# Turning more attention output by DMA, in a kernel whose order a planner writes

## The chip, the cores and the metric

The kernel runs on one core of a Trainium2 chip. A core has TensorE (PE, with its weight loads shown as PEld), VectorE (DVE), ScalarE (ACT), GpSimd (POOL) and SyncE (SP); POOL, SP and ACT also issue DMAs, which 16 DMA engines carry out. The metric is the device time of one execution in microseconds (us), of which the median over runs is compared.

## The reference

Two stages, the second fed by the first. Sizes: 8 batches, 8 heads, 576 positions, head width 64; then 4608 tokens, width 512, 8 experts, inner width 1024.

```python
def phi(x):
    proj = np.einsum('bhsd,df->bhsf', x, w_phi)
    proj = proj - np.max(np.abs(proj), axis=-1, keepdims=True)
    return np.concatenate([np.exp(proj), np.exp(-proj)], axis=-1)
q_p, k_p = (phi(q), phi(k))
kv = np.einsum('bhsf,bhsd->bhfd', k_p, v)
z = np.sum(k_p, axis=2)
num = np.einsum('bhsf,bhfd->bhsd', q_p, kv)
den = np.einsum('bhsf,bhf->bhs', q_p, z)[..., None] + 1e-06
attn_out = num / den
x = attn_out.transpose(0, 2, 1, 3).reshape(B * S, H * D)

logits = x @ w_gate
P = np.exp(logits - logits.max())
for _ in range(8):
    P /= P.sum(1, keepdims=True) + 1e-09
    P /= P.sum(0, keepdims=True) + 1e-09
    P *= N / E
for e in range(E):
    h = np.maximum(x @ w1[e], 0.0)
    out += P[:, e:e + 1] * (h @ w2[e])
```

## The kernel before

Every operation is first recorded in a `Plan`, with its engine, a duration and what it reads and writes; `Plan.schedule` then plays the record through. At each step it starts, of all operations that are ready, the one that can start first, and among equals the one with the lowest number (`idx`, its place in the record plus `plan.prio`). The order that comes out is the order of instructions in each engine's queue. On the chip each queue runs strictly in that order, and semaphores hold an instruction until what it reads is there. The planner's durations therefore set the order but not the times.

**Attention.** The 8 heads of a batch make 4 pairs, so there are 32 pairs, numbered 4 x batch + pair. The string `order` lists the steps of the attention, one letter each, in the order in which they are recorded:

- `l`, `e`: load halves of a batch, and its last 64 positions. From batch 2 on q and k come through POOL's queue.
- `t`: turn a half's q and k with a DMA transpose on SP's queue (L567, 512 KB). `r` does it for the last 64 positions (L686).
- `a`, `q`, `p`: project and take exponentials on ACT (L618), with the maxima on DVE (L614).
- `b`, `n`, `m`: sums over keys, then the quotient, on PE (L622, L905) and DVE (L913, L918, L919). The result of a pair is the tile `xb`.
- `c` (`pair_c`): turn `xb` so that tokens lie along the free axis, into `xT`. For batches 3 to 6 this is a DMA transpose of 128 KB on SP's queue (L928). For the others PE turns four 128x128 blocks (L934) and DVE copies the result from PSUM (L937).
- `g`: turn the last 64 positions of all four pairs on PE (L944), copy them (L949), and compute the gate's logits of the group of 512 tokens.
- `w`: load expert 0's weights in eight parts through POOL's queue (L527, L531).
- `u`, `d`: the expert work that fills the attention's gaps: expert 0's up product of a group with its relu on ACT (L983, tile `hx`), and its down product with a copy into `acc`.

Some tiles lie inside larger ones, and the profile shows the larger name: `wx` stands for part of the buffers of `xb`, `k` and others, too.

**Routing.** The eight normalisations are a chain on DVE, with one small matmul each (L622 `ps<-cs,colw`), while PE goes on with expert 0.

**Experts 1 to 7.** The products use Strassen-like sums: DVE forms sums of weights and of tokens (L1240), PE multiplies (L1475, L1607, L1466), ACT and DVE empty the banks (L1527, L1530, L1535, L1676, L1860, L1872), POOL adds into `acc` (L1875). For experts from 2 on some products are split once more; `fine_up` forms the finer weight sums (`step`, 256 elements each), into space inside `xT`. Sums of tokens are written to DRAM in expert 1's turn (L1385, L1422, L1450) and read back later (L1397). The order of the small units of work inside a turn is written out in `UNITS`, one line for each kind of turn.

The planner prices a DMA by two numbers: how long its queue is held, and how long the transfer takes:

```python
o = plan.op(queue, 0.8 if queue == "POOL" else 0.6, 0.0, fn, r, w, (), nbytes / speed)
o.turn, o.unit = rate == 148, unit
```

Of the kernel before, what the change touches and what calls it, by code (L numbers as in the profile page):

```python
# [12 lines left out]
ALU = mybir.AluOpType  # L13
# [113 lines left out]
class Links:  # L127
# [13 lines left out]
    def step(self, t, work):  # L141
        on = [n for n in range(2) if self.line[n] and self.line[n][0][0] <= t + 1e-9]
        later = [x[0][0] for n, x in enumerate(self.line) if x and n not in on]
        if not on:
            return (min(later), None, None) if later else None
        share = [1.0, 1.0]
        if len(on) == 2:
            a, b = (x[0][2] for x in self.line)
            all_ = (0.61 if a.turn else 0.84) / (a.unit + b.unit)
            share = [all_ * a.unit, all_ * b.unit]  # L150
        dt, n = min((work[n] / share[n], n) for n in on)
        if later and later[0] - t < dt:
            dt, n = max(later[0] - t, 0.0), None
        for i in on:
            work[i] -= dt * share[i]
        return t + dt, n, work
# [193 lines left out]
def kernel(  # L350
# [18 lines left out]
    NP = H // 2  # L369
# [40 lines left out]
    plan = Plan()  # L410
# [17 lines left out]
    def dma(queue, nbytes, rate, fn, r=(), w=()):  # L428

        speed, unit = LINK.get(rate, (rate, 40))  # L430
        if nbytes == 2 << 20:
            speed, unit = 400, 150
        o = plan.op(queue, 0.8 if queue == "POOL" else 0.6, 0.0, fn, r, w, (), nbytes / speed)
        o.turn, o.unit = rate == 148, unit

    TI, GR, KM, QM, PM, NM, RM = 0, 0, 0, 0, 0, 0, 0
# [69 lines left out]
    def new(tag):  # L506
        return R[tag].new()
# [416 lines left out]
        return xb, outs  # L924

    def pair_c(b, pr, xb):
        if b in (3, 4, 5, 6,):
            dma("SP", 1 << 17, 148, lambda: nc.sync.dma_start_transpose(  # L928
                out=xT[:, pr, b * SM:(b + 1) * SM].rearrange("p (a c) -> p a c", c=128),
                in_=xb()[:, 0:NJ].rearrange("p a b -> p (a b)")), [(xb, 0), (xb, 1)], [("xT", b, pr)])  # L930
            return
        pxt = new("PP")
        for j in range(NJ):
            pe(128, lambda j=j: nc.tensor.transpose(  # L934
                bf(pxt)[:, j * 128:j * 128 + 128], xb()[:, j, :], ident),
                [(xb, 0), (xb, 1), "ident"], [pxt])
        dve(270, lambda: nc.vector.tensor_copy(  # L937
            out=xT[:, pr, b * SM:(b + 1) * SM], in_=bf(pxt)[:, 0:512]),
            [pxt], [("xT", b, pr)])
# [91 lines left out]
    for b in range(2):  # L1031
# [4 lines left out]
        w=["wphi_f0"])  # L1036
    dma("ACT", 1 << 15, 100, lambda: nc.scalar.dma_start(out=wphi_f[64:128, :], in_=w_phi),
        w=["wphi_f1"])
# [13 lines left out]
    for i in range(2):  # L1052
        dve(450, lambda i=i: nc.vector.memset(vrd[i], 0.0),
            w=[("vrd", i, h, *y) for h in range(2) for y in ((), (1,))])
# [35 lines left out]
    def stage_g(b):  # L1090
# [9 lines left out]
             "c": lambda j: pair_c(j // 4, j % 4, xbs[j]), "g": stage_g,  # L1100
             "u": lambda i: up0(i // 4, i % 4), "d": lambda i: down0(i // 4, i % 4)}
    order = (
        "lraeaepqbwlqaqawwabwmqlltnrbppnwqbppmrmanbqaqmwwacmpnpbccpwbtcnmqnaqbclupunm"
        "taumquglcapalbcpnqqdcenmucugbblnapmrcqdutabnqpmunpbambccddnqplanmqmducpblttb"
        "augnaqlnrbdcampcadmqeutunqcppmdcaqtdqabpbbmlrqtdnpmuaqualbnagnacctbmqulupran"
        "tdpmtdqcmdnpdabdancpcabbqmpumqbcdgnappqunburqcbugmmnqdcdanumupqbnucmcpnmbddp"
        "bqmpncncubncmmgccg"
    )
    for i, n in enumerate(order):
        at[0] = i  # L1110
# [23 lines left out]
    o = plan.op("X", 0.0, 0.0, swap, w=["late"])  # L1134
# [136 lines left out]
    def fine_up(A, n):  # L1271

        f, r = A[n]
        t, key, first = FINE_W[n]

        def a(q, k):
            return lambda: f()[:, k, :].rearrange("p (f q c) -> p q f c", f=2, q=2)[:, q]

        def s(n):
            return lambda: t()[:, n]  # L1280

        def step(n, x, y, op, r, w):
            sub(dve, 256, s(n), x, y, op, r, [(key, n), *w])

        step(0, a(1, 0), a(1, 1), ALU.add, r, first)
        step(2, a(0, 0), a(1, 0), ALU.subtract, r, [])
        step(1, s(0), a(0, 0), ALU.subtract, [*r, (key, 0)], [])
        step(3, a(0, 1), s(1), ALU.subtract, [*r, (key, 1)], [])
        A[n + "*"] = t, [(key, i) for i in range(4)]
# [500 lines left out]

    def down7(e, g, H, B7):

# [131 lines left out]

    END = "X1 p2 Y1 X2 Z1 p3 X3 Z2 X4 p0 p1".split()
    UNITS = [o.split() for o in (
# [27 lines left out]
    turns = [int(i) for i in (  # L1954
        "0 1 2 3 4 5 6 7 8 9 10 11 12 13 14 15 16 17 9 10 11 12 13 14 15 16 17 9 10 11 12 "
        "13 14 15 16 17 9 10 11 12 13 14 15 16 17 9 10 11 12 13 14 15 16 17 18 9 10 11 12 "
# [22 lines left out]
    for e in range(1, E):  # L1979
        w1, w2 = load_w(e, ["late", ("acc", 4, 0, 0)] if e > 1 else ["late"])  # L1980
        if e == 1:
            nextX = sums_x(pairs[0])
        A7 = sums_up(e, w1)
        B7 = sums_down(e, w2) if e > 1 else None
        turn = [*pairs, (8,)] if e < E - 1 else [(8,), *pairs]
        if e == 2:
            o = plan.op("X", 0.0, 0.0, lambda: None, w=["K"])
            for d in plan.ops[:-1]:
                if any(b.ring is R["X"] for b in d.bufs):
                    d.users.append(o)  # L1990
                    o.deps.append(d)
                    o.left += 1
        for n, gs in enumerate(turn):
            if (e, n) == (1, 4):
                plan.inorder = 1
            X = nextX if e == 1 else load_fine(gs)
            H = {g: [] for g in gs}
            for fp in range(len(gs)):
                hs = take()
                for i, z in enumerate(hs):  # L2000
                    H[gs[min(i, len(gs) - 1)]].append(z)
                fine = e > 1 and len(gs) == 2
                if fine:
                    un = up49(A7, fp, X, H, gs, ["up0", "K"])
                else:
                    un = up7(A7, gs, fp, X, H, ["up0"])
                for o in UNITS[turns.pop(0)]:
                    if o in un:
                        un[o]()
                    elif len(o) == 3:  # L2010
                        un[o[:2], int(o[2])]()
                    elif dn is not None:
                        dn[o]()
                if dn is not None:
                    dn["out"]()
                    slots.extend(dn["slots"])
                if e == 1 and fp == 0 and n + 1 < len(turn):
                    nextX = sums_x(turn[n + 1], [(H[gs[0]][0], 0, 1, 1)])
                if B7 is None and fp:
                    B7 = sums_down(e, w2)  # L2020
                if fp == len(gs) - 1:
                    wait += [(e, g, H[g], B7, w2, [z.ring.number for z in H[g]]) for g in gs]
                dn = next_down()
# [35 lines left out]
```

## Time and profile before

| | |
|---|---|
| median of 3 runs | 1010.16 us (1009.79 to 1010.67) |
| profiled execution | span 1008.8 us from the first to the last instruction; its time outside the span is not listed, the median is 1.4 us above it |
| PE, PEld busy | 994.0 us (99%), 727.7 us (72%) |
| DVE, ACT, POOL busy | 898.6 us (89%), 812.8 us (81%), 447.6 us (44%) |
| granted TensorE clock | 1.000 |
| DMA | 128.86 MB, mean 128 GB/s |

Busy time of PE is the union of its matmuls, whose ends are modelled and overlap, so the time from one start to the next tells its pace better than the length of one. `SPq` is SP's queue: the time that an issuing instruction held it, waits included. A row of the windows table gives the length of a stretch, and for each engine the busy time in it and the number of instructions, then the granted clock, the DMA share (which counts overlapping queues, so it can exceed 1) and GB/s.

### The profile page before, as it was taken

The page shows a single profiled execution, that of the slowest core. Times are in us where ns is not written, and L with a number is a line of the kernel's source. Part 1 is how long each engine was busy: PE and PEld are TensorE (multiplying, and loading weights), DVE is VectorE, ACT ScalarE, POOL GpSimd, SP SyncE. Part 2 cuts the span into 40 slices and gives each one's busy share as a digit, 9 for nine tenths or more (in the row PEclk, how much of TensorE's full clock was granted, in tenths as well). Part 3 has the DMA queues.
Part 4 walks back from the last instruction along what each step waited for, and adds up shares of the span by engine and source line. Part 5 has one row for each costly group of instructions (what it writes and reads, how often), then busy time and mean ns, then how long its engine had stood idle before and what let it go on. Part 6 is the DMA issues. An engine that isn't in the chain of part 4 may idle for free.

```text
span 1008.8 us, 23309 instructions
## 1 busy us (share of the span) xinstructions
PE 994.0 (99%) x8376; PEld 727.7 (72%) x8376; DVE 898.6 (89%) x1999; ACT 812.8 (81%) x1930; POOL 447.6 (44%) x514
## 2 busy tenths in 40 slices
PE   7899999999999999999999999999999999999998
PEld 5666666644566877777777877787778777787775
DVE  7999998987888998899989898989889988989886
ACT  7999999845979788878878788777887888778874
POOL 5778674400133344434444444444443444344443
PEclk9999999999999999999999999999999999999999
DMA  9999999181136423282327133632246222724653
GB/s 249 183 202 183 157 153 144 38 170 56 53 121 143 147 97 98 84 184 96 109 98 170 44 100 131 130 127 98 97 117 177 97 98 84 147 79 142 208 174 126
DMA packets 129748, 128.86 MB, mean 128 GB/s; under 512 B 55776, under 2 KB 98272, under 8 KB 129632
## 3 DMA queue, kind: packets, MB, share of 16 engines
q1 hardware_dynamic: 97680, 103.33, 36.3%
q0 software_dynamic: 31648, 23.86, 16.9%
q8 instruction: 65, 1.06, 0.5%
q14 instruction: 51, 0.42, 0.2%
q10 hardware_dynamic: 304, 0.20, 0.1%
HBM read 122.50 MB, written 19.53 MB: 141 GB/s over the span
## 4 chain that ended last, share of the span: by engine, by line
PE 92%; DVE 3%; ACT 2%; DMA 2%; issue 1%; POOL 0%; DVEq 0%
PE ps L1466 41%; PE ps L1475 20%; PE ps L622 17%; PE ps L1607 11%; PE ps L905 2%; DMA xi6t<-X 1%; DMA xi<-X 1%; PE ps L752 1%; ACT q L618 0%; DVE m L614 0%; ACT k L618 0%; DVE wx L614 0%; DVE X L1240 0%; DMA acc<-in_k_dram 0%; DVE hs L1676 0%
## 5 line engine op out<-in xcount | busy, mean ns | idle before, releaser
L1875 POOL TENSOR_TENSOR acc<-acc,hx 128x512 f32<-128x512 f32 x186 | 236.1, 1276 | 404.7 <-ACT hx L1872 135.0
L1466 PEld LDWEIGHTS <-hs 128*128 128x128 bf16 x1984 | 194.1, 98 | 46.4 <-issue 0.2
L1872 ACT ACTIVATE hx<-ps,P 128x256 f32<-128x256 f32 x372 | 158.9, 483 | 53.4 <-PE ps L1466 52.0
L1860 DVE SCALAR_TENSOR_TENSOR acc<-ps,P,acc 128x256 f32<-128x256 f32 x372 | 162.2, 478 | 30.2 <-PE ps L1466 28.2
L1475 PE MATMUL ps<-xT,T 128*128 128x512 bf16 x608 | 171.0, 379 | 0.0
L1466 PEld LDWEIGHTS <-hx 128*128 128x128 bf16 x1488 | 145.6, 98 | 24.9
L1466 PE MATMUL ps<-hx,hs 128*128 128x256 bf16 x992 | 144.3, 273 | 0.0
L1676 DVE CUSTOM_DVE_ANT_0 hs<-ps,U 128x512 bf16<-128x512 f32 x192 | 124.7, 684 | 11.3 <-PE ps L1475 6.6
L1607 PE MATMUL ps<-xT 128*128 128x256 bf16 x576 | 125.4, 272 | 0.0
L1475 PEld LDWEIGHTS <-T 128*128 128x128 bf16 x672 | 65.8, 98 | 40.6
L1682 ACT ACTIVATE hs<-ps 128x512 bf16<-128x512 f32 x96 | 55.9, 598 | 41.7 <-PE ps L1475 40.2
L1466 PE MATMUL ps<-wx,hs 128*128 128x256 bf16 x560 | 78.4, 273 | 0.0
L622 PE MATMUL ps<-w,hx 128*128 128x512 bf16 x288 | 73.0, 379 | 0.0
L622 PE MATMUL ps<-xT,w 128*128 128x512 bf16 x288 | 72.9, 379 | 0.0
L1466 PE MATMUL ps<-wx,hx 128*128 128x256 bf16 x496 | 72.3, 273 | 0.0
L1676 DVE CUSTOM_DVE_ANT_0 hs<-ps,X 128x512 bf16<-128x512 f32 x96 | 65.1, 684 | 7.8 <-PE ps L1607 6.9
L1466 PE MATMUL ps<-hx 128*128 128x256 bf16 x496 | 71.2, 273 | 0.0
L1607 PEld LDWEIGHTS <-xT 128*128 128x128 bf16 x576 | 56.3, 98 | 17.5
L1466 PE MATMUL ps<-w,hx 128*128 128x256 bf16 x432 | 62.2, 273 | 0.0
L614 DVE TENSOR_REDUCE m<-ps 128x4 f32<-128x512 f32 x88 | 58.8, 680 | 3.7 <-PE ps L622 1.9
L1672 ACT COPY X<-ps 128x512 f32<-128x512 f32 x96 | 58.6, 610 | 2.5 <-DVE ps L1650 2.5
L1466 PE MATMUL ps<-w,hs 128*128 128x256 bf16 x432 | 60.2, 273 | 0.0
(174 smaller groups left out, 2256.0 us busy)
## 6 DMA issues: line engine op xcount, KB each, us to landing
xT<-xi SPq DMA_DIRECT2D x48, 448.0 KB, 4.6
xT<-xd SPq DMA_DIRECT2D x72, 256.0 KB, 4.0
wx<-in_moe_w_dram POOLq DMA_DIRECT2D x8, 1024.0 KB, 11.2
v_m<-in_v_dram SPq DMA_DIRECT2D x15, 512.0 KB, 5.2
out_dram<-acc SPq DMA_DIRECT2D x14, 512.0 KB, 3.0
w<-in_moe_w_dram POOLq DMA_DIRECT2D x6, 1024.0 KB, 11.0
xT<-xp SPq DMA_DIRECT2D x24, 256.0 KB, 2.8
qk<-in_k_dram POOLq DMA_DIRECT2D x12, 256.0 KB, 5.4
```

The costliest lines, as they stand in the source:

```text
L614: dve(el, lambda: nc.vector.tensor_reduce(out=dst(), in_=src(), axis=AX.X, op=ALU.max, apply_absolute_value=True), r, w)
L622: nc.tensor.matmul(out_, lhsT=lhsT, rhs=rhs, start=start, stop=stop)
L905: pe(65, lambda j=j: nc.tensor.matmul(pn()[:, j * D1:j * D1 + D1], lhsT=s["T"][x]()[:, j % 2, 2 * h + j // 2, :] if j < 4 else r["T"][x]() ...
L1466: pe(256, lambda i=i, k=k, z=z: nc.tensor.matmul(bank()[:, 256 * i:256 * i + 256], lhsT=lhs(k, i), rhs=rhs(k), start=first and z, stop=k = ...
L1475: pe(512, lambda k=k: nc.tensor.matmul(bank().rearrange("p (a b) -> p a b", a=2), lhsT=lhs(k), rhs=rhs(k), start=first and k == 0, stop=k ...
L1607: pe(256, lambda: nc.tensor.matmul(halves_of(bank[q], n)(), lhsT=lhs(), rhs=t()[:, rhs, :], start=start, stop=True, skip_group_check=True) ...
L1672: act(512, lambda: nc.scalar.copy(out=flat(to[q])(), in_=bank[q]()), [bank[q]], [(to[q], 0), (to[q], 1)])
L1676: dve(515, lambda: nc.vector._custom_dve(ADD_SAT, out=out_(q, i, j), in0=bank[q]().rearrange("p (a b) -> p a b", a=2), in1=to[q](), s0=3.0 ...
L1682: act(512, lambda: nc.scalar.activation(out=out_(q, i, j), in_=bank[q]().rearrange("p (a b) -> p a b", a=2), func=ACT.Relu, bias=0.0, scal ...
L1860: dve(320, lambda n=n, ts=ts: nc.vector.scalar_tensor_tensor(out=acc[g][:, ts, 256 * j:256 * j + 256], in0=bank()[:, 256 * n:256 * n + 256 ...
L1872: act(370, lambda n=n: nc.scalar.activation(out=u()[:, n, :], in_=bank()[:, 256 * n:256 * n + 256], func=ACT.Copy, bias=0.0, scale=P[:, 4 ...
L1875: pool(695, lambda: nc.gpsimd.tensor_tensor(out=acc[g][:, 2 * i:2 * i + 2, 256 * j:256 * j + 256], in0=acc[g][:, 2 * i:2 * i + 2, 256 * j: ...
```

## The change

Four edits.

1. The planner now holds SP's queue for 2.8 us for a turn of 512 KB and for 1.25 us for a smaller one, where it held 0.6 us.
2. `pair_c` turns all pairs by DMA but 0 to 3, 6 and 7: 26 of 32 where it was 16. Newly turned by DMA are pairs 4 and 5 (batch 1), 8 to 11 (batch 2) and 28 to 31 (batch 7).
3. The `order` string and all 19 lines of `UNITS` are other permutations of the same steps and units. The weight sums of expert 2 (`sums_up`, `fine_up`) get numbers lower by 300, so that they win ties against the rest.
4. In `fine_up` the third sum also waits for the space in `xT` to be free.

```diff
-        o = plan.op(queue, 0.8 if queue == "POOL" else 0.6, 0.0, fn, r, w, (), nbytes / speed)
+        issue = 0.8 if queue == "POOL" else 0.6
+        if rate == 148:
+            issue = 2.8 if nbytes == 1 << 19 else 1.25
+        o = plan.op(queue, issue, 0.0, fn, r, w, (), nbytes / speed)
         o.turn, o.unit = rate == 148, unit
...
     def pair_c(b, pr, xb):
-        if b in (3, 4, 5, 6,):
+        if NP * b + pr not in (0, 1, 2, 3, 6, 7):
             dma("SP", 1 << 17, 148, lambda: nc.sync.dma_start_transpose(
...
     order = (
-        "lraeaepqbwlqaqawwabwmqlltnrbppnwqbppmrmanbqaqmwwacmpnpbccpwbtcnmqnaqbclupunm"
+        "laapqewrqlaqewabwablbqwpnlmqbpcmrntmpraqbnwnaqppanmcpcbtwmcnbwpacqwqnlmuluua"
...
         step(0, a(1, 0), a(1, 1), ALU.add, r, first)
-        step(2, a(0, 0), a(1, 0), ALU.subtract, r, [])
+        step(2, a(0, 0), a(1, 0), ALU.subtract, r, first)
...
     UNITS = [o.split() for o in (
-        "x10 X1 x11 Y1 w10 Z1 Z2 X2 x21 x20 X3 w11 x30 x40 X4 y11 x31 w20 x41 y10 w21",
+        "x10 w10 y10 x11 X1 x21 X2 Z1 x20 w11 X3 Z2 w21 Y1 x31 w20 y11 x30 X4 x40 x41",
...
+        plan.prio = -300 if e == 2 else 0
         A7 = sums_up(e, w1)
+        plan.prio = 0
```

More of the change, by code (lines that the diff above doesn't have):

```diff
@@ L1102 @@
     order = (
-        "lraeaepqbwlqaqawwabwmqlltnrbppnwqbppmrmanbqaqmwwacmpnpbccpwbtcnmqnaqbclupunm"
[L1104 to L1107, printed above, removed]
+        "laapqewrqlaqewabwablbqwpnlmqbpcmrntmpraqbnwnaqppanmcpcbtwmcnbwpacqwqnlmuluua"
+        "mqbpmltuabgadalpbeccncmnucmupqqnptubgbaqrdnaqpquamtmpblnddccqapblpanmbtmddqn"
+        "pmdacbmrnuuatpgeqbubncnnmlctqpcbdlmudacclrnadpmqtbgutqlbndcpamatqucbanuqqapm"
+        "mcbubarundpqdmbpnqqdtpddanpmamqubgapqqurbncuanpbcdncmcmubadpmccbcqbungpqucmn"
+        "pdncbmdpnmncmucgcg"
     )
```

52 rows, old and new, of the table UNITS are left out of this document.

## The prediction

> **What bounds the kernel.** I read the page first: span, busy times, slices, and the summary of the chain that ended last.
>
> ```profile
> span 1008.8 us, 23309 instructions
> PE 994.0 (99%) x8376; PEld 727.7 (72%) x8376; DVE 898.6 (89%) x1999; ACT 812.8 (81%) x1930; POOL 447.6 (44%) x514
> PEclk9999999999999999999999999999999999999999
> DMA  9999999181136423282327133632246222724653
> PE 92%; DVE 3%; ACT 2%; DMA 2%; issue 1%; POOL 0%; DVEq 0%
> ```
>
> PE is busy in 994.0 of 1008.8 us at full clock, and 92% of the last chain is PE. Whether PE is truly full I take from the pace of matmuls in the chain (start, length, count):
>
> ```profile
> 81.53 1.73 PE ps L622 x8
> 331.61 17.47 PE ps L1466 x160
> 1001.93 3.06 PE ps L622 x22
> ```
>
> Eight matmuls of 512 columns take 1.73 us, 0.216 each; 160 of 256 columns take 17.47, 0.109 each: the same time per column early and late, with nothing between them. So PE is the bound, and only two things can move the end: PE work, and the time in which PE stands still. The windows table (length; PE, PEld, DVE, ACT, POOL busy with counts; clock, DMA share, GB/s) shows where it stands still:
>
> ```profile
> 0.00:64.00 64.00, 54.27 (x594) 37.77 (x595) 57.88 (x127) 58.31 (x145) 45.28 (x80) 1.00 1.17 216
> 64.00:196.00 132.00, 132.00 (x1524) 86.24 (x1523) 121.11 (x278) 127.38 (x312) 86.80 (x138) 1.00 0.98 145
> 196.00:245.00 49.00, 48.64 (x335) 24.09 (x334) 42.31 (x122) 20.45 (x39) 1.94 (x4) 1.00 0.44 94
> 245.00:350.00 105.00, 104.37 (x713) 69.60 (x712) 90.45 (x216) 89.87 (x179) 29.45 (x23) 1.00 0.43 122
> 350.00:1009.00 659.00, 654.70 (x5216) 509.99 (x5213) 586.81 (x1260) 516.83 (x1260) 284.15 (x271) 1.00 0.41 119
> 24.00:32.00 8.00, 6.99 (x81) 4.86 (x79) 7.88 (x19) 7.96 (x22) 5.50 (x10) 1.00 1.22 254
> 48.00:56.00 8.00, 7.63 (x101) 5.27 (x98) 7.96 (x21) 8.00 (x22) 7.81 (x12) 1.00 1.21 187
> ```
>
> PE idles 9.73 us in the first 64 us, 0.36 from 196 to 245, 0.63 from 245 to 350, and 4.30 after that, of which 4.0 follow the last matmul (1001.93 + 3.06 = 1004.99). Beyond the start there is one microsecond to win back. In the start ACT and DVE are full (7.96 and 7.88 of 8 us; 8.00 and 7.96), so PE waits for them. And from 64 to 196 us, the attention's main part, ACT is busy 127.38 of 132: PE and ACT are both nearly full there.
>
> **The change part by part.** The order listing of both programs shows what is issued: 40 transposes on PE and 10 copies on DVE fewer, 10 DMA transposes on SP more; all else has the same counts.
>
> The PE transposes. A timeline has one pair's four, and what follows:
>
> ```profile
> 194.06 0.39 PE L934 MATMUL ps<-ident,xb 128*128 128x128 bf16 x4
> 194.29 0.81 PE L622 MATMUL ps<-xT,w 128*128 128x512 bf16 x3
> ```
>
> From start to next start 0.23 us a pair, so ten pairs free 10 x 0.23 = 2.3 us of PE. On a full PE that is worth 2.3. The Trainium skill (Perfetto Trace Analysis, Identifying the Most-Contended Engine) says that matmul busy share misleads because matmuls overlap, and that weight-load busy and MFU tell the headroom instead. By its measure, 72% here, over a quarter of PE would be free, and the 2.3 us might be worth nothing; the pace above contradicts that, and rival B holds what is left of it.
>
> How much of the 2.3 arrives depends on where it falls. Pairs 28 to 31 come at the end of the attention, where ACT has 20.45 us of work in 49: their 0.9 us arrives whole. Pairs 4, 5 and 8 to 11, 1.4 us, fall where ACT is nearly full. In both orders ACT's last attention exponential is its instruction 456, with the same work ahead of it, so that end can move forward only out of ACT's 4.62 us of idle (132 - 127.38). That is over 1.4, but some of it is latency. Bounds: lose 0 or all 1.4; I take a loss of 0.4, nearer to zero as the idle is three times what is asked.
>
> The DVE copies and the SP and DMA work that replaces them:
>
> ```profile
> L937 DVE COPY xT<-ps x16: 384/415/426, 41.2 to 202.7; 128x512 bf16<-128x512 bf16 x16
> L928 SPq DMA_TRANSPOSE xT<-xb x10: 1189/1195/1723, 94.5 to 188.4; - x10
> DMA to landing us min/median/max: 2.3/4.6/7.2
> L567 SPq DMA_TRANSPOSE qkT<-qk x12: 1324/2438/5192, 42.6 to 170.2; - x12
> DMA to landing us min/median/max: 4.3/5.8/10.3
> ```
>
> (Each landing line is for the turns in the row above it; the first covers all sixteen of L928.) Ten copies by 0.415 free 4.2 us of DVE, which is not the bound: zero. Ten turns by 1.195 hold SP for 12 us spread over some 140; SP computes nothing, so also zero, as long as nobody waits for what is queued behind a turn. The cover is distance: a turn needs 2.3 to 7.2 us to land where the copy took 0.4, and `xT` must be read later than that. For the last pair I count it. In the changed order 19 expert matmuls of 512 columns (4.1 us) and some small ones stand between PE's last L905 and the gate of group 7, 4.8 us in all. The chain beside it is a reciprocal, the quotient, and a turn on quiet DMA engines:
>
> ```profile
> 201.36 0.49 DVE L919 TENSOR_TENSOR wx<-ps,wx 128x320 bf16<-128x320 f32 x1
> L928 SPq DMA_TRANSPOSE xT<-xb x1: 1190/1190/1190, 188.4 to 188.4; - x1
> DMA to landing us min/median/max: 2.3/2.3/2.3
> ```
>
> 0.2 + 0.5 + 2.3 plus handovers, some 3.3 us: covered by 1.5. If that cover fails, each microsecond costs one, up to 3.4 (a landing of 7.2).
>
> The new issue times are not on the chip; they only move orders. At the start, 349 matmuls still stand ahead of PE's first expert-0 matmul, and 107 ACT instructions ahead of the first relu: the same work on full engines. One thing differs. In the chain before, POOL issues two weight loads just ahead of a product that DVE and PE wait for:
>
> ```profile
> 27.41 1.16 POOL L527 DMA_DIRECT2D w<-in_moe_w_dram  x2
> 28.57 1.93 POOL L810 TENSOR_TENSOR v<-v_m,em 128x1024 bf16<-128x1024 f32 x1
> ```
>
> In the changed queue one stands there (0.58 less), but three loads and the other weight part now stand a little earlier. Bounds 0 to -0.6; I take -0.2.
>
> Expert 2's weight sums, now preferred. The one large stall behind the start lies there:
>
> ```profile
> 317.00 7.75 DMA xi6t<-X
> 326.46 0.69 DVE L1240 TENSOR_TENSOR T<-w 128x1024 bf16<-128x1024 bf16 x1
> 328.33 0.28 DVE L1240 TENSOR_TENSOR xT<-w 128x256 bf16<-128x256 bf16 x1
> 328.53 0.68 DVE L1530 CUSTOM_DVE_ANT_0 hs<-ps,U 128x512 bf16<-128x512 f32 x1
> 330.20 1.19 PE L1475 MATMUL ps<-X,wx 128*128 128x512 bf16 x4 [0.62 <-DVE hs L1530]
> ```
>
> A store of 7.75 us holds DVE up, then 2.07 us pass from the first weight sum to the add (L1530) that frees PE's bank. In the changed queue eight sums of 256 (0.20 us from start to start, by the row before the add) instead of one, and two accumulating reads of PSUM (L1860, priced like two such sums each), stand in between: 7 x 0.20 + 4 x 0.20 = 2.2 us more. Against that PE has other products ahead of that point. Bounds: the stall of 0.62 goes, or it grows by 2.2; I take +0.2. The extra wait in `fine_up` is on reads that the first sum, just ahead, awaits already: zero. The permuted `UNITS` keep all counts; before, PE's idle from 350 us to its last matmul is 0.3: between -0.3 and, for a few seams of the 0.62 kind, +1.5; I take 0.
>
> Sum: -2.3 + 0.4 - 0.2 + 0.2 = -1.9 us. The profiled span, 1008.8, goes to 1006.9; the median has 1.36 us around that: 1010.16 - 1.9 = 1008.3. A measurement of this kernel tells about 0.2%, 2.0 us, from no change, so below 1008.1 is faster and above 1012.2 slower.
>
> **The rivals.**
>
> A, the forecast: bounds, with every part at its end, 1010.16 - 2.3 - 0.6 - 0.6 - 0.3 = 1006.4 and 1010.16 - 2.3 + 1.4 + 2.2 + 1.5 = 1013.0; most of it between 1007 and 1010. Chance 0.48, half of it on either side of 1008.1.
>
> B, ACT is the bound of the attention. Then the 1.4 us come back as waits of PE for L618, and only the end's 0.9 stays: 1010.16 - 0.9 = 1009.3. For it speaks ACT at 96% from 64 to 196 with unchanged work, against it PE at 132.00 of 132.00. Chance 0.13.
>
> C, the slower one: SP's queue. It is strictly in order, and an `xT` turn waits at its head for `xb`:
>
> ```profile
> SPq L928 <- DVE m L614: 28.0, 9, 7.2
> PE ps L752 <- DMA acc<-in_k_dram: 4.0, 1, 4.0
> ```
>
> (Total, times, longest.) Before, all sixteen stand behind the sixth qkT turn; changed, five stand ahead of it, at 45 to 95 us, where the DMA slices read 9. A qkT turn held up, or landing after the worst 10.3 instead of 5.8 us, comes 4.5 us late, and PE, whose order is fixed, waits at its first `wphi,qkT` matmul: 1010.16 - 1.9 + 4.5 = 1012.8. It decides once a turn lands behind that matmul. Against it: after the start no wait of PE for a DMA is listed (the second row is the first load), and planning with true issue times moves turns forward. The Trainium skill (VectorE: DVE Perf Modes, The three transpose paths and its rules) gives 390 ns for a 128x128 transpose on TensorE and 1309 by DMA, and prefers TensorE where PSUM will do. By that, an estimate, forty tiles would cost 36.8 us more if they lay on the path; four in 0.23 us on PE and the SP rows say that they overlap and lie beside it, so I weigh it only as lateness here. Chance 0.19.
>
> D, everything gained: 2.3, the stalls of 0.62 and 0.36, and 0.6 at POOL: 1010.16 - 3.9 = 1006.3. For it speaks that little idle needs to vanish, against it that each order has seams of its own. Chance 0.20.
>
> That the turns are not issued is excluded by the counts.
>
> **How the numbers follow.** Faster: half of A and D, 0.44. Same: half of A and B, 0.37. Slower: C, 0.19. The range reaches from just under D to short of C's 1012.8: 1005.8 to 1012.3; outside it lie the worse half of C and some of D.
>
> **What would show it.** Right: PE busy shrinks, by the modelled ends, by some two microseconds and idle after 64 us stays near 5; L934 has 24 matmuls; L928 has 26 turns that nobody waits for. A is wrong if PE shows waits for L618 between 64 and 196 (B), for DMA `qkT` or `xT` (C), or over 1.5 us at L1475 near 330; and all of this is wrong if the first 64 us change by over a microsecond, for I hold them fixed.

## The result, and the profile after

| | before | changed |
|---|---|---|
| median | 1010.05 us (1009.72 to 1010.93, 6 runs) | 1018.46 us (1014.4 to 1021.54, 6 runs) |
| profiled execution | 1010.16 us, span 1008.8 us | 1018.4 us, span 1016.6 us |

The ratio is 1.0084, 95% interval 1.0068 to 1.0099: the change makes the kernel 8.4 us slower, where 2 us faster was forecast. The changed kernel also scatters: its runs lie 7 us apart, those of before 1.2.

The page of the changed kernel:

```profile
span 1016.6 us, 23170 instructions
PE 990.9 (97%) x8298; PEld 724.7 (71%) x8336; DVE 898.2 (88%) x1989; ACT 811.9 (80%) x1930; POOL 446.1 (44%) x514
PE 87%; DMA 5%; ACT 3%; POOL 2%; DVE 2%; issue 1%; POOLq 0%; DVEq 0%
```

PE has less work and holds a smaller part of the chain; 5% of the chain are now DMAs. The windows table tells where PE stands (columns as in the prediction):

```profile
0.00:64.00 64.00, 52.45 (x594) 36.52 (x600) 57.86 (x128) 58.01 (x144) 45.33 (x80) 1.00 1.12 214
64.00:196.00 132.00, 124.87 (x1402) 81.72 (x1423) 114.86 (x261) 121.38 (x300) 83.44 (x134) 0.99 0.95 152
196.00:245.00 49.00, 47.28 (x353) 24.28 (x358) 39.20 (x114) 24.97 (x48) 5.01 (x8) 1.00 0.49 105
245.00:350.00 105.00, 103.63 (x678) 66.22 (x678) 92.52 (x215) 83.99 (x168) 25.66 (x21) 1.00 0.42 122
```

In the main part of the attention, 132.00 of 132.00 before, PE is busy 7.1 us less; in the start 1.8 less and from 196 to 245 us 1.4. (The trace of the changed kernel lacks some matmul records, so PE's count is 38 below that of its weight loads; the waits are the safer measure.) PE's waits from 50 to 350 us (total, times, longest), then POOL's row for the same turns, then SP's rows:

```profile
PE ps L625 <- POOL wx L819: 4.2, 1, 4.2
PE ps L625 <- DMA qkT<-qk: 1.7, 2, 1.0
PE ps L625 <- DVE cs L1182: 1.3, 1, 1.3
PE ps L1469 <- DVE acc L1863: 1.3, 1, 1.3
PE ps L625 <- POOL r L873: 0.4, 1, 0.4
```

```profile
POOL qk L553 <- DMA qkT<-qk: 8.2, 3, 4.9
```

```profile
L570 SPq DMA_TRANSPOSE qkT<-qk x12: 1317/3720/6792, 41.8 to 166.5; - x12
DMA to landing us min/median/max: 4.3/7.1/10.9
```

(Lines lie three further down than before: L570 is the qkT turn, L553 the q and k loads on POOL, L931 the xT turn, L625 the former L622.) PE's waits sum to 9.3 us with two small ones of 0.2, where before they were 1.3. POOL, which before waited for no qkT turn, now does so for 8.2 us, and the median landing of a qkT turn went from 5.8 to 7.1 us. The largest stall in the chain of waits, and POOL's queue beside it:

```profile
140.92 8.87 DMA qkT<-qk
151.15 0.76 POOL qk L553
151.91 1.93 POOL wx L813
153.91 0.26 POOL wx L819
154.21 1.04 PE ps L625 x16
```

```profile
145.26 0.23 POOL L811 TENSOR_SCALAR wx<-wx 128x8 f32<-128x8 f32 x1 [1.84 <-DVE wx L617]
150.34 0.81 POOL L553 DMA_DIRECT2D qk<-in_k_dram  x1 [4.85 <-DMA qkT<-qk]
151.15 0.76 POOL L553 DMA_DIRECT2D qk<-in_q_dram  x1
151.90 1.94 POOL L813 TENSOR_TENSOR wx<-v_m,wx 128x1024 bf16<-128x1024 f32 x1
```

A qkT turn issued at 140.9 us took 8.87 us. The next pair of q and k loads reuses the buffer that this turn reads, so POOL stood at that load for 4.85 us, its product of v (L813) stood behind it in the queue, and PE needed the product. Before, each such load came 1.9 us or more after its turn had landed, and the last pair 10.8 us after. After the stall PE ran at half pace for a while (granted clock 0.53, then 1.00):

```profile
154.20:157.60 3.40, 3.17 (x22) 1.83 (x23) 1.03 (x2) 3.27 (x10) 3.24 (x5) 0.53 0.95 220
157.60:161.00 3.40, 3.40 (x39) 2.25 (x38) 3.08 (x7) 2.27 (x7) 1.86 (x6) 1.00 0.70 131
```

That is, by estimate, 3.4 x 0.47 = 1.6 us more. The account: 8.0 us more of waits and 1.6 of slow clock, less 2.3 of transposes that went, make 7.3 of the 7.8 by which the span grew.

### The profile page after: what moved, and what is told of

Read it like the earlier page. It is cut to its first block, busy times and chain, and to the rows that moved or that the text cites. A ratio compares the mean times of both kernels' runs of the same rounds, so it can differ in the third digit from the quotient of the medians.

```text
span 1016.6 us, 23170 instructions
## 1 busy us (share of the span) xinstructions
PE 990.9 (97%) x8298; PEld 724.7 (71%) x8336; DVE 898.2 (88%) x1989; ACT 811.9 (80%) x1930; POOL 446.1 (44%) x514
## 4 chain that ended last, share of the span: by engine, by line
PE 87%; DMA 5%; ACT 3%; POOL 2%; DVE 2%; issue 1%; POOLq 0%; DVEq 0%
PE ps L1469 41%; PE ps L1478 20%; PE ps L625 14%; PE ps L1610 11%; DMA qkT<-qk 3%; PE ps L908 1%; DMA xi<-X 1%; DMA xi6t<-X 1%; ACT wx L621 1%; ACT k L621 1%; POOL wx L813 1%; ACT q L621 0%; POOL qk L553 0%; DVE X L1243 0%; DMA acc<-in_k_dram 0%
## 5 line engine op out<-in xcount | busy, mean ns | idle before, releaser
L1875 ACT ACTIVATE hx<-ps,P 128x256 f32<-128x256 f32 x372 | 162.8, 488 | 39.1 <-PE ps L1469 34.6
L1863 DVE SCALAR_TENSOR_TENSOR acc<-ps,P,acc 128x256 f32<-128x256 f32 x372 | 162.3, 476 | 20.6 <-PE ps L1469 17.7
L1469 PE MATMUL ps<-hx,hs 128*128 128x256 bf16 x992 | 147.7, 272 | 1.4 <-DVE acc L1863 1.3
L1679 DVE CUSTOM_DVE_ANT_0 hs<-ps,U 128x512 bf16<-128x512 f32 x192 | 125.0, 683 | 10.2 <-PE ps L1478 3.3
L1610 PE MATMUL ps<-xT 128*128 128x256 bf16 x576 | 128.5, 272 | 0.1
L625 PE MATMUL ps<-xT,w 128*128 128x512 bf16 x271 | 70.1, 379 | 1.0 <-DVE xb L922 0.2
L625 PE MATMUL ps<-w,hx 128*128 128x512 bf16 x276 | 70.0, 382 | 0.6 <-issue 0.2
L1615 ACT COPY ps<-ps 128x256 f32<-128x256 f32 x144 | 54.6, 379 | 11.2 <-PE ps L1610 10.6
```

The source lines that it names most:

```text
L625: nc.tensor.matmul(out_, lhsT=lhsT, rhs=rhs, start=start, stop=stop)
L1469: pe(256, lambda i=i, k=k, z=z: nc.tensor.matmul(bank()[:, 256 * i:256 * i + 256], lhsT=lhs(k, i), rhs=rhs(k), start=first and z, stop=k = ...
L1610: pe(256, lambda: nc.tensor.matmul(halves_of(bank[q], n)(), lhsT=lhs(), rhs=t()[:, rhs, :], start=start, stop=True, skip_group_check=True) ...
L1615: act(293, lambda: nc.scalar.copy(out=halves_of(bank[q], n)(), in_=halves_of(bank[q2], n2)()), [bank[q2]], [bank[q]])
L1679: dve(515, lambda: nc.vector._custom_dve(ADD_SAT, out=out_(q, i, j), in0=bank[q]().rearrange("p (a b) -> p a b", a=2), in1=to[q](), s0=3.0 ...
L1863: dve(320, lambda n=n, ts=ts: nc.vector.scalar_tensor_tensor(out=acc[g][:, ts, 256 * j:256 * j + 256], in0=bank()[:, 256 * n:256 * n + 256 ...
```

## The experiments

The theories. Q: attention loses what late qkT turns pass on through POOL's queue. Q1: it is the ten added turns that make them late. Q2: it is the new order of steps, which puts loads and turns together. M, J: the loss is in the expert stage. G: the last four pairs' turns delay what follows the attention.

| run | median, us (runs) | ratio to before, 95% |
|---|---|---|
| e1 expert edits taken back | 1027.02 (4) | 1.0166 (1.0151 to 1.0182) |
| e2 16 turned pairs | 1022.32 (4) | 1.0120 (1.0105 to 1.0135) |
| e3 before, 26 turned pairs | 1033.12 (4) | 1.0233 (1.0200 to 1.0266) |
| e4 last loads 4 later | 1014.72 (5) | 1.0046 (1.0031 to 1.0061) |
| e5 loads before them 3 later | 1018.57 (4) | 1.0080 (1.0063 to 1.0097) |
| e6 last loads 10 later | 1012.51 (7) | 1.0027 (1.0016 to 1.0038) |
| e7 three pairs of loads later | 1012.49 (10) | 1.0033 (1.0019 to 1.0047) |
| e8 before, expert edits alone | 1010.95 (10) | 1.0009 (0.9999 to 1.0018) |
| e9 before, ten turns as load | 1018.60 (4) | 1.0086 (1.0071 to 1.0101) |
| e10 plain copies | 1021.05 (4) | 1.0104 (1.0087 to 1.0121) |
| e11 e6, last four pairs on PE | 1010.90 (10) | 1.0009 (1.0000 to 1.0018) |
| e12 e11, one more load later | 1014.78 (4) | 1.0044 (1.0029 to 1.0059) |
| e13 no DMA for the ten | 1020.86 (4) | 1.0098 (1.0075 to 1.0120) |
| e14 before, pairs 28, 29 turned | 1010.40 (11) | 1.0002 (0.9993 to 1.0011) |
| e15 e9, v load first | 1021.62 (4) | 1.0114 (1.0098 to 1.0129) |
| e16 e9, loads 5 later | 1017.18 (4) | 1.0071 (1.0054 to 1.0088) |
| e17 e9, both | 1018.50 (4) | 1.0084 (1.0067 to 1.0101) |

### Parts taken back or added alone: e1, e2, e3, e8

e1: `UNITS`, `fine_up` and the -300 as before, in the changed kernel.

> The changed kernel with the three edits that touch the expert stage taken back: UNITS, the fourth wait of fine_up and the weight of -300 are those of before; the issue times, the 26 turned pairs and the order of steps stay. Theory Q (the loss lies in the attention stage: qkT turns land late, POOL waits for one in order and PE behind POOL): the 4.4 us stall at 150 us and its half-clock tail stay, the two longer waits at 229 and 337 us (1.0 and 0.7 us more than before) go or stay, so 1016 to 1019 us. Theory M (the loss is made in the expert stage): 1008 to 1011 us.

e2, in the changed kernel:

```diff
-        if NP * b + pr not in (0, 1, 2, 3, 6, 7):
+        if b in (3, 4, 5, 6,):
```

> The changed kernel with only 16 pairs turned by DMA, as before; the order of steps, the issue times and the expert stage stay the new ones. Theory Q1 (it is the ten added xT turns that make the qkT turns land late): the median landing of qkT falls from 7.1 to about 5.8 us, the stall at 150 us goes, PE does 40 transposes (2.3 us) more, so 1010 to 1013 us. Theory Q2 (it is the order of steps, which puts loads and turns together, whatever the number of turns): the landing stays near 7 us and the time at 1017 to 1021 us.

e3, in the kernel before, is the same edit the other way round.

> The kernel before with only the 26 turned pairs added; old order of steps, old issue times, old expert stage. Theory Q1 (the turns themselves): qkT lands late here too, stalls of several us in attention, 1013 to 1020 us. Theory Q2 (the order of steps): the turns lie behind other work, 40 transposes go, 1007.5 to 1010 us.

e8: the three expert edits of the change in the kernel before.

> The kernel before with the three edits of the expert stage alone: new UNITS, the fourth wait of fine_up, the weight of -300. Attention keeps its turns, its orders and its issue times. Theory J (UNITS are fitted to the state in which attention leaves the engines, and cost in any other): stalls of 5 to 12 us between 350 and 600 us, as the old UNITS had behind the new attention (8 us more there), 1015 to 1022 us. Rival (the orders of UNITS move filler among streaming matmuls, as the prediction had it): 1009.5 to 1011.5 us.

The first three are all slower than the changed kernel itself, outside what either theory gave. They cannot price their parts: the planner writes every queue anew, so each compares two orders. What their traces show is that the parts hang together. With 26 turned pairs and the old `UNITS` PE stands still for 3.3 us (e1) and 5.2 us (e3) between 350 and 400 us, where the changed kernel's PE never does; the rows are that stretch of the changed kernel, e1, and e3:

```profile
350.00:400.00 50.00, 50.00 (x405) 39.44 (x403) 45.20 (x102) 42.39 (x105) 21.61 (x21) 1.00 0.21 66
```

```profile
350.00:400.00 50.00, 46.74 (x342) 33.90 (x340) 40.13 (x91) 35.21 (x84) 18.05 (x17) 0.93 0.16 49
```

```profile
350.00:400.00 50.00, 44.84 (x320) 32.34 (x318) 38.96 (x87) 31.34 (x76) 14.62 (x14) 0.90 0.17 51
```

So with 26 turned pairs the old expert edits lose time there; which of the three it is, no run tells. On the kernel before the new ones cost little: e8 is 0.7 us above it, with an interval that just holds no change, and J falls there. M falls too: e1 keeps the stall at 150 us (5.3 us).

### The stall at 150 us: e4, e6, e5, e7

These keep every queue of the changed kernel but POOL's, in which one or three pairs of q and k loads move. With n the pair and k the number of POOL instructions to pass, this is e6:

```diff
         done = self.schedule()
+        for n, k in ((11, 10),):
+            two = self.loads[2 * n:2 * n + 2]
+            at = done.index(two[0])
+            done = [o for o in done if o not in two]
+            pool = [i for i, o in enumerate(done) if i >= at and o.eng == "POOL"]
+            done[pool[k - 1] + 1:pool[k - 1] + 1] = two
```

e5 has (10, 3), e7 (4, 3), (10, 3), (11, 10). e4 moves pair 11 past the next four POOL instructions that are no DMAs.

> The changed kernel with one pair of instructions moved in one queue: the last two qk loads on POOL (at 150.3 us, waiting 4.9 us for a qkT turn) stand behind the four POOL operations that followed them instead of ahead; every other engine's order is the same. Theory Q (PE's 4.4 us at 149.8 is POOL's wait for the turn, passed on in order): that stall goes with its half-clock tail of 1.3 us, 1012 to 1014.5 us. Rival (the stall is one of several parallel lateness chains, the next one takes its place): 1016 to 1019 us.

> The run with the last qk loads moved, taken further: they stand behind ten POOL operations instead of four, so that the scaled values of the rests (vrd) too are made before POOL waits for the turn. In the run with four the stall became 2.5 us at 154.3 with POOL vrd as its end. Theory Q (PE loses what POOL's wait in order passes on, and nothing else stands behind it): no stall over 0.6 us between 130 and 170 us, 1011.5 to 1013.5 us. Rival (the loads are now so late that the last half's turn is): a stall for qkT near 165 us, 1014 to 1017 us.

> The changed kernel with one other pair moved on POOL: the two qk loads issued at 141.5 and 142.4 us (which run beside the qkT turn issued at 140.9, landing after 8.9 us) stand behind the three short POOL operations that followed them, at about 145.5 us; all other orders are the same. Theory L (the turn is late because the two loads share the DMA engines with it): the turn lands within 4.5 to 6.5 us, the next pair of loads waits for it by less than 1.5 us instead of 4.9, and most of the 4.4 us stall of PE and its tail goes: 1013 to 1015.5 us. Rival T (a turn of 512 KB in this stage takes 7 to 10 us with or without them): it lands after 8 us or more and the stall stays, 1017 to 1020 us.

> Three pairs of qk loads moved behind short POOL operations that followed them (the pairs at 75.7, 141.5 and 150.3 us, behind 3, 3 and 10 operations). Theory Q: the stall of 0.6 us at 77 us goes as well, so 0.5 us less than with the last pair alone, 1011 to 1013 us; what is left over before is the wait for the first turns at 51 and 74 us (1.2 and 0.9 us) and the two waits at 229 and 337 us (1.0 and 0.7 us more than before), less 2.3 us of transposes. Rival (each load put off makes the turn behind it later): 1014 us or more.

e4 took 3.7 us off and left a stall of 2.4 us, at POOL's next product (`vrd`), which still stood behind the load. e6 went past that too: 1012.51, 6.0 us below the changed kernel, as theory Q had it, and POOL's wait for a turn is gone from its list between 130 and 170 us. That one pair of loads, in its place in POOL's queue, held 6.0 of the 8.4 us. PE's three longest waits in e6 from 50 us on (eight lines inserted, so L633 is L625):

```profile
PE ps L633 <- DMA qkT<-qk: 1.6, 2, 1.1
PE ps L1477 <- DVE acc L1871: 1.3, 1, 1.3
PE ps L633 <- DVE cs L1190: 1.2, 1, 1.2
```

e5 missed: the turn landed after 7.5 us instead of 8.9, with the two loads issued 5.4 us after it instead of 0.6, and the stall fell to 2.2 us, but the profiled run had 3.2 us of wait for the very first turn at 51 us, where the other runs have 0 to 1.1 with the same orders, and the median did not move. Why this turn takes so long, when its counterpart before landed after 4.3 us, stays open. e7 gained nothing over e6: the stall at 77 us went, and a wait of 1.9 us came at 100, for a turn of the last positions (`rT`).

### Turns or orders: e9, e10, e13

e9 prices the turns alone, in the old orders: SP issues the ten new turns where PE turns the pair, into a tile that nobody reads.

```diff
         pxt = new("PP")
+        if NP * b + pr not in (0, 1, 2, 3, 6, 7):
...
+            first = lambda: (nc.sync.dma_start_transpose(
+                out=spare[n].rearrange("p (a c) -> p a c", c=128),
+                in_=xb()[:, 0:NJ].rearrange("p a b -> p (a b)")), nc.tensor.transpose(
+                bf(pxt)[:, 0:128], xb()[:, 0, :], ident))[1]
...
```

> The kernel before, every order kept, with the ten turns of the changed kernel added on SP beside the transposes that PE still makes: each added turn writes a buffer that nobody reads, so nothing waits for it, and no work goes. It prices the ten turns as mere load on SP and on the DMA engines. Theory Q2 (the loss comes from where the new order of steps puts loads and turns): 1009.5 to 1012 us. Theory Q1 (ten more turns make the qkT turns land late): stalls of several us before 200 us, 1013 to 1020 us.

e10 and e13 keep the new orders and put a plain DMA copy, or a copy on DVE, in the place of the ten turns:

```diff
-            dma("SP", 1 << 17, 148, lambda: nc.sync.dma_start_transpose(
+            start = nc.sync.dma_start_transpose if b in (3, 4, 5, 6) else nc.sync.dma_start
+            dma("SP", 1 << 17, 148, lambda: start(
...
+                nc.vector.tensor_copy(
+                    out=xT[:, pr, b * SM:(b + 1) * SM],
+                    in_=xb()[:, 0:NJ].rearrange("p a b -> p (a b)")),
```

> The changed kernel, every order kept, with a plain copy of the same 128 KB in the place of each of the ten added turns (so those parts of xT are not transposed in this run). Theory Q1 (the turning itself crowds the DMA engines): the qkT turn issued at 140.9 us and the first two land 2 us or more earlier, the stalls before 170 us shrink by half, 1011 to 1014 us. Theory Q2 (order): the turn at 140.9 still lands after 8 to 9 us, the stall at 150 us stays, 1016 to 1019 us.

> The changed kernel, every order kept, without the ten added turns: a copy on DVE of the same 128 x 512 elements stands where SP issued each (so those parts of xT are not transposed in this run); SP and the DMA engines are free of them. Theory N (the ten turns make the loss in the new orders too): the stalls before 170 us shrink to 1 us or less, 1009 to 1012 us. Theory O (the new orders put loads right behind the turns they wait for, whatever else SP issues): the qkT turn at 140.9 still lands after 8 us or more and PE stalls 3 to 5 us there, 1014 to 1018 us.

Each theory holds in one pair of orders: Q1 in the old ones, and Q2 in the new ones for the stall at 150 us. In the old orders ten turns that nobody waits for cost 8.8 us (Q1). The POOL wait and the turn behind it:

```profile
POOL qk L553 <- DMA qkT<-qk: 7.1, 1, 7.1
```

```profile
95.02 7.57 DMA qkT<-qk
```

In the kernel before that turn was issued at 91.16 and took 4.3 us; here two added turns stand ahead of it on SP, it is issued 3.9 us later, beside two loads of POOL, and takes 7.6: PE stands for 6.6 us there and has a clock of 0.55 for the 3.4 us behind it, by estimate 8.1 of the 8.8. In the new orders the stall comes from the orders (Q2): with plain copies the turn at 141 still takes 9.5 us, and with no DMA at all for the ten pairs 9.1, with 4.3 us of POOL's wait and 3.7 of PE's:

```profile
140.19 9.07 DMA qkT<-qk
151.38 1.93 POOL wx L813
153.68 1.32 PE ps L625 x19
```

The medians of e10 and e13, 1021.05 and 1020.86, lie above what either theory gave. e13's runs scatter (1016.7 to 1023.0; the profiled one is the fastest), and ten copies on DVE were added, so its median is no price; that the stall stays is what it tells. What the ten turns cost in the new orders is therefore not priced.

### The last pairs: e11, e12, e14

e11 is e6 with pairs 28 to 31 on PE again; its orders are those of e6 up to 180 us. e12 also puts off the fourth pair of loads (3, 4).

```diff
-        if NP * b + pr not in (0, 1, 2, 3, 6, 7):
+        if NP * b + pr not in (0, 1, 2, 3, 6, 7, 28, 29, 30, 31):
```

> The changed kernel with the last qk loads behind ten POOL operations (1012.5 us by itself) and the last four pairs (28 to 31) turned on PE again; up to 180 us its orders are the same. Theory G (the turn of the last pairs delays the last gate matmuls, the routing behind them and the first sums: 0.8 us at 229 and 0.5 to 0.7 us at 337): both stalls go back to the size of before (0.5 and 0.8 us), 0.9 us of transposes come back, 1011.5 to 1012.5 us. Rival (the stalls come from the new UNITS or the weight of -300): they stay, 1013 to 1014 us.

> The run with pairs 28 to 31 on PE and the last loads put off, and the fourth pair of qk loads (at 61.7 us) also put off behind four POOL operations, to about 66 us. If the qkT turn issued at 67 us lands late (8.1 us) because these loads run beside it, it lands within 6 us, the stall of 0.9 us at 74 us goes, 1010.5 to 1012 us. Rival (the turn behind the put-off load is late in its place): a stall near 80 us, 1012 to 1014 us.

e14, in the kernel before:

```diff
-        if b in (3, 4, 5, 6,):
+        if b in (3, 4, 5, 6,) or NP * b + pr in (28,29):
```

> The kernel before with two more pairs turned by DMA, 28 and 29, which come at about 190 us, where the DMA engines are nearly idle. Eight transposes go (0.44 us by the 0.055 us each that PE took). Theory: where nothing queues behind SP, a turn costs nothing, 1009.4 to 1009.9 us against 1010.1. Rival (the turns delay the first expert transfers on SP, as in the changed kernel): 1010.2 to 1011.5 us.

e11, at 1010.90, is 1.6 us below e6, although PE does 0.9 us of transposes more. Its two late waits shrink, the second well and the first a little (e6: 1.2 and 1.3):

```profile
PE ps L633 <- DVE cs L1190: 0.9, 1, 0.9
PE ps L1477 <- DVE acc L1871: 0.4, 1, 0.4
```

So with these four pairs on PE the kernel is faster, by more than theory G gave. That the turns delay what follows them, as G has it, is not shown. The two waits fall by 1.2 us together, which pays for the 0.9 us of transposes and little more; PE's waits for the first turns are also smaller in e11's profile. And e11's queues are planned anew behind 180 us: ACT's order differs in 21 places. e13 tells more, for it keeps the changed kernel's orders and turns none of these pairs by DMA:

```profile
PE ps L1473 <- DVE acc L1867: 1.3, 1, 1.3
PE ps L625 <- DVE cs L1186: 0.7, 1, 0.7
```

The wait at 337 us is as long there as in the changed kernel, so it comes from the order and not from the turns. The one at 229 is 0.6 us shorter, so some of it may be theirs.

e12 missed: the turn that was to be freed took 11.1 us, with the loads put off beside it, and PE waited 3.1 us for it at 73. e14 is no different from before: two turns where the DMA share is low (0.29 from 170 to 200 us in the kernel before) neither pay nor cost what can be measured; its profiled span (1007.5) is 1.3 us shorter, but that run is the fastest of eleven. No version beat the kernel before.

### What carries the ten turns' cost in the old orders: e15, e16, e17

All three are e9 with single moves. e15 puts the v load that stands behind the turn issued at 95.0 ahead of it on SP; e16 moves the waiting loads (7, 5) on POOL as above; e17 does both.

```diff
         done = self.schedule()
+        i = done.index(self.turned[5])
+        j = next(j for j in range(i + 1, len(done)) if done[j].eng == "SP")
+        done.insert(i, done.pop(j))
```

> The kernel before with the ten added turns as load (1018.6 us), and one instruction moved on SP: the v_m load issued at 100.6 us stands ahead of the qkT turn issued at 95.0 (whose issue took 5.5 us) instead of behind it. Theory S (SP's queue in order is the carrier: v_m is issued 7.5 us later than in the kernel before, POOL's v waits for it and PE for POOL): v_m lands near 100 us, the stall of 6.8 us at 100 shrinks to 1 to 2.5 us, 1012.5 to 1015 us. Rival E (the DMA engines are full, whoever comes first): the qkT turn is later by as much and PE waits for it instead, 1016.5 to 1019 us.

> The kernel before with the ten added turns as load (1018.6 us), and the eighth pair of qk loads on POOL (at 103.1 us, after a wait of 7.1 us for the qkT turn issued at 95.0) put off behind the five POOL operations that followed it. Theory P (the same carrier as in the changed kernel: a qkT turn that lands late holds POOL at the load that reuses its buffer, and the v product behind it holds PE): the stall of 6.8 us at 100 us goes, what is left over the kernel before is 1 to 1.5 us at 235 and 338 us, 1011 to 1013 us. Rival (PE would have waited for v_m or for the late turn itself anyway): a stall of 3 us or more near 100 us stays, 1015 to 1019 us.

> The kernel before with the ten added turns as load (1018.6 us), and both moves: the v_m load ahead of the qkT turn on SP, and the eighth pair of qk loads on POOL behind the five operations that followed it. Theory PS (one late turn holds two queues, SP at its issue and POOL at the load that reuses its buffer, and either alone is enough to hold POOL's v product): the stall near 100 us shrinks to 1.5 us or less, 1011 to 1013.5 us. Rival (the DMA engines are full in this stage, so that something else lands late there): a stall of 3 us or more between 95 and 130 us, 1015 to 1018 us.

None brought the time down by more than 1.5 us, and all are slower than their theories gave. e15 is 3.0 us slower than e9, above its rival too: POOL waited 10.0 us for the turn and PE 9.7 us for POOL, so the move made the turn later, as rival E had it. e16: the wait for the turn went and POOL waited 6.2 us for the v load instead, which SP could issue only after the turn's issue had held it for 5.9 us. e17: both waits shrank, and two stalls of 1.8 us at 107 and 3.0 at 119 stayed or came, each with one of POOL's loads in its chain: the rival. So in the old orders taking one wait away brings another. A reason may be in the windows of the kernel before: from 64 to 130 us the DMA share is above 1, and only from 170 on is it low.

```profile
64.00:90.00 26.00, 26.00 (x306) 17.25 (x305) 24.84 (x59) 25.02 (x62) 19.32 (x30) 1.00 1.32 184
90.00:130.00 40.00, 40.00 (x453) 26.06 (x452) 37.19 (x84) 38.05 (x95) 28.34 (x47) 1.00 1.20 170
170.00:200.00 30.00, 30.00 (x404) 20.25 (x401) 27.79 (x71) 27.72 (x67) 14.59 (x24) 1.00 0.29 54
```

That full DMA engines are the cause is argued from this and from e17, not shown by a run of its own.

## Why the prediction was wrong

**The bound** was right: PE streams, and only its idle time could move the end. So was the gain: 40 transposes went, and the account above closes with their 2.3 us.

**The step that failed** is the one on SP and DMA work: "Ten turns by 1.195 hold SP for 12 us spread over some 140; SP computes nothing, so also zero, as long as nobody waits for what is queued behind a turn." Zero was 8.8 us in the old orders (e9), most of it where two added turns pushed a qkT turn 3.9 us back. The condition was named and its check was wrong: I counted who waits for an xT turn, not what a turn does to the transfers beside and behind it. The DMA slices, which read 9 up to 176 us, were weighed only for rival C.

**The second step that failed** was left unsaid: that the new order of steps is free because counts are the same. I followed turns past turns on SP, and not POOL's loads, which stand in the new order right behind the turn that frees their buffer. This is the larger part of the 8.4 us: one pair of them cost 6.0 (e6), and the wait behind it is there without the ten turns too, 4.3 us on POOL and 3.7 on PE (e13).

**The last pair**, "covered by 1.5 us": no wait of PE for xT is listed, so that cover held. What failed is that these pairs were to give 0.9 us "whole": with them on PE again the kernel is 1.6 us faster (e11). The two waits of PE at 229 and 337 us, which grew from 0.4 and 0.6 to 1.3 each, explain little of that; through what else the four turns, or the orders planned around them, cost more than they save stays open.

**Expert 2's weight sums**, +0.2 within -0.6 to +2.2: the wait of 0.6 us for L1530 is gone, and PE waits 1.3 us at 337 for the accumulating reads (`acc`, L1863), in front of which DVE makes eight sums of 256, as the prediction had them. That is 0.7 us more. With the expert edits alone this wait is 0.6 us (e8), in e11 0.4, and with the changed orders and none of the ten turns 1.3 (e13): it depends on the order behind the attention, not on the weight alone and not on the turns. **`UNITS` and `fine_up`**, 0 within -0.3 to +1.5: all three expert edits together cost 0.7 (e8), inside the bounds.

**The start** was to stay within a microsecond. PE's waits before 64 us sum to 10.2 us where they were 8.8, 1.0 of it the wait for the first qkT turn at 51 us, which ran from 0 to 3.2 us among runs with the same orders there. Among the changed kernel's own runs it may be a part of the scatter; what sets its size in a run stays open.

**The rivals.** B is out: no wait of PE for L621 between 64 and 196. D is out. C named the right thing, a qkT turn 4.5 us late and PE waiting, and its price was 4.5 of the 8.4. But its carrier was an xT turn at the head of SP; the trace has POOL's queue, held by a load behind the late turn. Its chance, 0.19, rested on two arguments that fell. No wait of PE for a DMA before: a wait of POOL for one is enough. True issue times move turns forward: planned with the old ones, the changed kernel has one neighbouring pair on SP the other way round and every other queue in the same order. The page of the Trainium skill on transposes that was weighed there (VectorE: DVE Perf Modes, The three transpose paths and its rules) prefers TensorE. In the old orders a run agrees with its direction (e9), not through its 1309 ns, since an xT turn, four such tiles, landed in 2.3 us on quiet DMA engines, but through what a turn does to others.

## What to carry to other kernels

Before work goes to a queue that computes nothing, read how full the DMA engines are in that stage, and count every transfer that lands later for it. In these traces a load that reused a buffer held its whole queue until the last reader was done (4.85 us on POOL), so look at what stands behind such a load, on queues off the path too: moving one pair of loads behind the work that followed it was worth 6.0 of the 8.4 us lost here. Orders fitted to one set of operations can't be judged, nor parts of them priced, by taking one set back: freeze all queues and move single instructions.

## What the runs showed of the hardware

- A qkT turn of 512 KB landed later the more of POOL's loads were in flight beside it. Over the 204 turns in seventeen profiles (before, changed, e1 to e15) the median landing was 4.4 us with no POOL load in flight at any time of the turn (35 turns), 7.2 with two (89) and 8.8 with four (19). A longer turn also meets more loads, so part of this goes the other way round; counted at the turn's issue alone the medians are 5.0 us without a load (87) and 7.8 with any (117). The Trainium skill (DMA: Bandwidth & Descriptors, Queues, rings and completion order) says that each DMA engine goes round its queues packet by packet; the trace agrees as far as turns were slower beside loads.
- The issue of such a turn held SP for 1.3 to 6.8 us in the changed kernel's profile. Over the same 204 turns the median was 1.9 us where at most one other transfer was in flight at the issue (43 turns) and 4.2 where three or more were (122). A plain copy of 128 KB held SP for 0.5 us where a turn held it for 1.2.
- After PE had waited 4.2 us its clock was 0.53 for 3.4 us. The Trainium skill (TensorE: Matmul & The Clock Gate, What's actually happening) says that an idle window of about 3.4 us halves the clock; the trace agrees here, and by that estimate the wait of 4.2 us cost 5.8. The length of a wait alone doesn't tell: after one of 3.7 us (e13) the clock stayed at 1.00, and after one of 2.4 us (e4) it was 0.50 for 3.4 us.
